# Attention windows and a highway layer on one core: the rectified product of eight tiles read by ScalarE, and a new order of the last two tiles

## The chip, the cores and the metric

The kernel runs on one core of a Trainium2 chip. The metric is the device time of one execution in microseconds (us), as the median of several runs. Five engines of the core work side by side, each through its own instructions in order: TensorE (PE in the profile, with its weight loads as PEld), VectorE (DVE), ScalarE (ACT), GpSimd (POOL) and SyncE (SP, here for stores only). They wait for one another through semaphores.

## The reference

Four batches of eight heads attend over 768 positions with 64 values a head. A position sees itself, the 127 before it, and the first four positions (the "sinks"). The heads' outputs, side by side, are the rows `x` of a highway layer:

```
scores = where(keep, scale * q @ k.T, -1e9)
x = softmax(scores) @ v                      # 3072 rows x 512
H = np.maximum(x @ w_h, 0.0)
T = 1.0 / (1.0 + np.exp(-(x @ w_t + b_t)))
out = T * H + (1.0 - T) * x
```

## The kernel before

The 3072 rows are 24 tiles of 128 rows, `N = 24`, six (`NC`) to a batch. All eight heads of a tile are worked on together. The last line of the reference is computed as `T * (max(h, 0) - x) + x`, where `h = x @ w_h`.

One tile goes through these steps, each a small function of the tile's number `n`:

- `scores(n)`: PE multiplies keys and queries into the PSUM tile `ps_s` (L303). `expo(n)`: ACT writes the exponentials to the fp16 tile `E` (L334). `mask(n)`: DVE multiplies `E` by a mask of ones and zeros (L342).
- `values(n)`: PE multiplies `E` of this tile and of the tile before by the values into `ps_v` (L371 and L374). A tile that begins a batch has no tile before it in its batch, so it has only the eight products of L374; the others have sixteen products, L371 and L374 in turn. L374 reads what `mask(n)` wrote.
- `norm(n)`: DVE takes reciprocals of the sums (L383) and writes the fp16 tile `X` (L384).
- `x_transpose(n)` on PE (L411) and `x_copy(n)` on ACT (L416) give the transposed rows `XT`.
- `bias(n)` and `gate(n)`: PE forms `x @ w_t + b_t` in `ps_z` (L421, L425). `tanh(n)`: ACT writes `TH = tanh(ps_z / 2)` (L449). The sigmoid is `0.5 * TH + 0.5`; that step is done on ACT by `gate_on_act` (L455) for the tiles that `on_act` names, and on POOL by `gate_value` (L460) for the others.
- `hidden(n)`: PE forms `x @ w_h` in `ps_h` (L465), in four products.
- `diff(n)`: one DVE instruction with `ps_h` and `X` as inputs writes `DD = max(ps_h, 0) - X` (L469). `gated(n)`: DVE multiplies `DD` by `TH` (L473). `add(n)`: POOL adds `X` (L477). `store(n)`: SP sends the tile to memory (L481).

The order of the work on every engine is the order in which the program is written. A loop at L657 makes one turn for each `s` from 5 to 21, and a turn works on five tiles at once, `n2 = s + 2` down to `n8 = s - 2`. In a turn, each engine's order is:

- PE: transposes of tile `n0 = s`, the last two products of `hidden(n9)` with `n9 = s - 1`, the scores of `n2`, the bias of `n0`, the values of `n1 = s + 1`, `gate(n0)`, the first two products of `hidden(n0)`.
- ACT: `x_copy(n0)`, `gate_on_act(n9)` where it is ACT's, `expo(n2)`, `tanh(n0)`.
- DVE: `mask(n1)`, `gated(n8)`, `diff(n9)`, `norm(n1)`, and in the turns 7 to 18 a transposition of query or key tiles (L155).
- POOL: `add(n8)`, `gate_value(n9)` where it is POOL's, in some turns the sink tables (L264, L280), and the loads that it issues (L130, L161).

In what follows "turn 12" means `s = 12`.

After the loop, the tiles 22 (`n0`) and 23 (`n1`) are finished by a sequence written out by hand (L705 to L747). The last tile is worked on in two halves of 256 columns, and its second half goes another way: two DVE instructions (L743, L745) and a store issued by ACT (L747).

Of the kernel before, what the change touches and what calls it, by code (L numbers as in the profile page):

```python
# [12 lines left out]
AF = mybir.ActivationFunctionType  # L13
ALU = mybir.AluOpType
# [16 lines left out]
def kernel(  # L31
# [14 lines left out]
    pe, act, dve, pool, sp = nc.tensor, nc.scalar, nc.vector, nc.gpsimd, nc.sync  # L46
# [10 lines left out]
    N = B * NC  # L57
# [237 lines left out]
    def scores(n):  # L295
        b, c = divmod(n, NC)
        nq = 2 if c + 1 < NC else 1
        new = n not in ADDED
        for hg in range(HG):
            for e in range(2):  # L300
                for g in range(G):
                    rows = slice(32 * g, 32 * g + 32)
                    pe.matmul(ps_s[:, g, hg, 0:nq * P],  # L303
                              lhsT=tr[b][rows, 1, hg, c * P:(c + 1) * P, e],
                              rhs=tr[b][rows, 0, hg, c * P:(c + nq) * P, e],
                              start=(new and e == 0), stop=(e == 1),
                              skip_group_check=not new)
# [16 lines left out]
    def sinks(b):  # L324
        sink_scores(b)
        sink_expo(b)
# [3 lines left out]
    def expo(n):  # L330
        c = n % NC
        nq = 2 if c + 1 < NC else 1
        E[n] = work.tile([P, G, HG, 2 * P], FP16, tag="E", name="E")
        act.activation(out=E[n][:, :, :, 0:nq * P], in_=ps_s[:, :, :, 0:nq * P],  # L334
                       func=AF.Exp, scale=SCALE)

    def mask(n):
        c = n % NC
        nq = 2 if c + 1 < NC else 1
        m = mask_0 if c == 0 else mask_std  # L340
        e3 = E[n].rearrange("p g hg x -> p (g hg) x")[:, :, 0:nq * P]
        return dve.tensor_tensor(  # L342
            out=e3, in0=e3, in1=m[:, 0:nq * P].unsqueeze(1).to_broadcast([P, H, nq * P]),
            op=ALU.mult)
# [7 lines left out]
    def values_of_sinks(n):  # L352
        b, t = divmod(n, NC)
        if t >= 2:
            rows = slice(32 * (t - 2), 32 * (t - 1))
            for i in range(2):
                pe.matmul(av_of(n)[:, i], lhsT=es[b % 2][rows],
                          rhs=vs[b][rows, HB * i:HB * i + HB, :].rearrange("p h e -> p (h e)"),
                          start=True, stop=False, skip_group_check=True)

    def values(n):
        b, t = divmod(n, NC)
        both = av_of(n)
        for i in range(2):
            for j in range(HB):
                h = HB * i + j
                g, hg = divmod(h, HG)
                slot = both[:, i, j * (D + 1):(j + 1) * (D + 1)]
                first = t < 2 and j == 0
                if t > 0:  # L370
                    pe.matmul(slot, lhsT=E[n - 1][:, g, hg, P:2 * P], rhs=v_of(n - 1)[:, h, :],  # L371
                              start=first, stop=False, skip_group_check=True)
                    first = False
                pe.matmul(slot, lhsT=E[n][:, g, hg, 0:P], rhs=v_of(n)[:, h, :],  # L374
                          start=first, stop=True, skip_group_check=True)

    X = [None] * N
# [12 lines left out]
    ALL = slice(0, DM)  # L390
    HALVES = [slice(0, DM // 2), slice(DM // 2, DM)]

    def z_of(n, cols):
        return ps_z[:, cols] if n < N - 1 or cols == HALVES[1] else ps_v[:, 0, cols]

    def h_of(n, cols):
        if n < N - 1 or cols == HALVES[1]:
            return ps_h[:, cols]
        return ps_s[:, 1].rearrange("p hg x -> p (hg x)")[:, cols]
# [6 lines left out]
    def flat(x):  # L406
        return x.rearrange("p i j d -> p (i j d)")

    def x_transpose(n):
        for kc in range(KC):  # L410
            pe.transpose(xt_of(n)[:, kc * P:(kc + 1) * P], flat(X[n])[:, kc * P:(kc + 1) * P],  # L411
                         ident)

    def x_copy(n):
        XT[n] = work.tile([P, KC * P], FP16, tag="XT", name="XT")
        act.copy(out=XT[n], in_=xt_of(n))  # L416

    def bias(n, cols=ALL, group=None):
        lhsT, rhs = (ones, brow) if group is None else (
            ones_g[32 * group:32 * group + 1], brow[32 * group:32 * group + 1])  # L420
        pe.matmul(z_of(n, cols), lhsT=lhsT, rhs=rhs[:, cols], start=True, stop=False)  # L421

    def gate(n, cols=ALL, parts=range(KC)):
        for kc in parts:
            pe.matmul(z_of(n, cols), lhsT=XT[n][:, kc * P:(kc + 1) * P], rhs=wt[:, kc, cols],  # L425
                      start=False, stop=(kc == KC - 1))

    TH = [None] * N
    DD = [None] * N
# [4 lines left out]
    def outputs(n):  # L434
        TH[n] = work.tile([P, DM], FP16, tag="TH", name="TH", bufs=6)
        DD[n] = work.tile([P, DM], FP16, tag="DD", name="DD", bufs=8)
        if O[n] is None:
            O[n] = work.tile([P, DM], FP32, tag="O", name="O", bufs=10)

    def on_act(n):  # L440

        return n < 6 or n in (8, 9, 12, 15, N - 3, N - 1)

    def at_once(n):

        return n < 6

    def tanh(n, cols=ALL, gate_too=True):
        act.activation(out=TH[n][:, cols], in_=z_of(n, cols), func=AF.Tanh, scale=0.5)  # L449
        if gate_too:  # L450
            gate_on_act(n, cols)

    def gate_on_act(n, cols=ALL):
        if on_act(n):
            act.activation(out=TH[n][:, cols], in_=TH[n][:, cols], func=AF.Copy, bias=0.5,  # L455
                           scale=0.5)

    def gate_value(n):
        if not on_act(n):
            pool.tensor_scalar(out=TH[n], in0=TH[n], scalar1=0.5, scalar2=0.5,  # L460
                               op0=ALU.mult, op1=ALU.add)

    def hidden(n, cols=ALL, parts=range(KC)):
        for kc in parts:
            pe.matmul(h_of(n, cols), lhsT=XT[n][:, kc * P:(kc + 1) * P], rhs=wh[:, kc, cols],  # L465
                      start=(kc == 0), stop=(kc == KC - 1))

    def diff(n, cols=ALL):
        dve.scalar_tensor_tensor(out=DD[n][:, cols], in0=h_of(n, cols), scalar=0.0,  # L469
                                 in1=flat(X[n])[:, cols], op0=ALU.max, op1=ALU.subtract)  # L470

    def gated(n, cols=ALL):
        return dve.tensor_tensor(out=DD[n][:, cols], in0=DD[n][:, cols], in1=TH[n][:, cols],  # L473
                                 op=ALU.mult)
# [182 lines left out]
    for s in range(5, N - 2):  # L657


        n2, n1, n0, n9, n8 = s + 2, s + 1, s, s - 1, s - 2  # L660
        x_transpose(n0)
        x_copy(n0)

        hidden(n9, parts=range(2, KC))
        if n2 % NC == 3:
            sinks(n2 // NC)
        if not at_once(n9):
            gate_on_act(n9)

        scores(n2)  # L670
        bias(n0, group=(n1 % NC + 1) % G)
        values_of_sinks(n1)
        expo(n2)

        if n1 not in ADDED:
            mask(n1)
        gated(n8)
        diff(n9)
        outputs(n0)
        values(n1)  # L680
        gate(n0, parts=range(0, 2))
        norm(n1)

        last = add(n8)
        while done < stored.get(n2, 0):
            store(done, after=last)
            done += 1
        gate_value(n9)
        if n2 in keys:
            sink_keys(keys[n2])  # L690
        if n2 in rows:
            sink_values(rows[n2], engine=pool)
        for load in loads[n2]:
            load()
        for piece in pieces[n2]:
            transpose_qk(*piece)
        for part in tiles[n2]:
            transpose_tiles(*part)
        if n2 == N - 1:
            mask(n2)  # L700
        gate(n0, parts=range(2, KC))
        tanh(n0, gate_too=at_once(n0))
        hidden(n0, parts=range(0, 2))

    n1, n0, n9, n8 = N - 1, N - 2, N - 3, N - 4  # L705
# [12 lines left out]
    gated(n9)  # L718
    finish(n9)
    gate(n0)  # L720
    tanh(n0)
    hidden(n0, parts=range(0, 1))
    x_transpose(n1)
    x_copy(n1)
    hidden(n0, parts=range(1, KC))
    gate_value(n0)
    diff(n0)
    gated(n0)
    finish(n0)
# [3 lines left out]
    for i, cols in enumerate(HALVES):  # L733
        gate(n1, cols)
        tanh(n1, cols, gate_too=(i == 0))
        hidden(n1, cols)
    diff(n1, HALVES[0])
    gated(n1, HALVES[0])
    finish(n1, HALVES[0])

    cols = HALVES[1]
    diff(n1, cols)
    dve.scalar_tensor_tensor(out=DD[n1][:, cols], in0=TH[n1][:, cols], scalar=1.0,  # L743
                             in1=DD[n1][:, cols], op0=ALU.add, op1=ALU.mult)
    dve.scalar_tensor_tensor(out=O[n1][:, cols], in0=DD[n1][:, cols], scalar=0.5,  # L745
                             in1=flat(X[n1])[:, cols], op0=ALU.mult, op1=ALU.add)
# [36 lines left out]
```

## Time and profile before

| what | us |
|---|---|
| median of 3 runs (110.75, 110.85, 113.58) | 110.85 |
| the profiled execution, its own time | 112.34 |
| its span from the first instruction to the last | 110.6 |
| DVE busy in the span | 94.9 |
| PE busy in the span | 97.8 |
| POOL busy in the span | 82.4 |
| ACT busy in the span | 79.4 |

The profiled execution's time has 1.74 us outside of its span, and it is 1.49 us above the median. The granted clock of TensorE has a mean of 0.975 of full speed over the span.

Each row of a timeline gives the start and the length in us, the engine, the line of the kernel, the operation, what is written `<-` what is read with shapes and types, the count, and in brackets how long the engine was idle before it and what ended the idle time. The rows of one engine can overlap by some 0.08 us, since the end of one instruction's writes lies beside the beginning of the next; the distance from start to start is then what an instruction costs its engine. The chain of waits goes back from the last instruction of the span to what released it, step by step.

### The profile page before, as it was taken

How to read it: one execution, taken by the hardware profiler on the slowest of the kernel's cores; microseconds unless marked ns; L12 is line 12 of the kernel's file. 1: busy time of each engine (PE TensorE's matmuls, PEld its weight loads, DVE VectorE, ACT ScalarE, POOL GpSimd, SP SyncE). 2: the span in 40 equal slices, each digit the busy share in tenths (PEclk: the TensorE clock that was granted, in tenths of full speed). 3: DMA queues.
4: the chain of work that ended last, by engine and by line, in shares of the span. 5: the costliest groups of instructions: out<-in, count | busy, mean ns of one | idle time of the engine just before them, and what ended most of it. 6: DMA issues, size and time to landing. Idle time of an engine off the chain costs nothing.

```text
span 110.6 us, 3031 instructions
## 1 busy us (share of the span) xinstructions
PE 97.8 (88%) x1199; PEld 51.4 (46%) x1199; DVE 94.9 (86%) x182; ACT 79.4 (72%) x105; POOL 82.4 (74%) x115
## 2 busy tenths in 40 slices
PE   5999777389999999899989999999999999999900
PEld 2344353246353654465445445655454555564600
DVE  5899889463989879999999999999989999899580
ACT  0934799806545989988959889988698879965700
POOL 6989995137989987689989799877995335664750
PEclk9999999967999999999999999999999999999996
DMA  3999999998999997999999999997999953345432
GB/s 95 251 211 168 141 183 165 184 202 131 119 168 166 126 144 68 152 106 115 128 121 94 162 273 154 171 267 160 186 150 203 232 190 115 121 147 191 182 128 69
DMA packets 45045, 17.53 MB, mean 158 GB/s; under 512 B 38500, under 2 KB 41316, under 8 KB 45032
## 3 DMA queue, kind: packets, MB, share of 16 engines
q0 software_dynamic: 40624, 9.97, 95.7%
q1 hardware_dynamic: 3944, 6.73, 17.1%
q10 hardware_dynamic: 464, 0.66, 2.2%
q8 instruction: 9, 0.15, 0.6%
q14 instruction: 4, 0.03, 0.1%
HBM read 21.01 MB, written 6.29 MB: 247 GB/s over the span
## 4 chain that ended last, share of the span: by engine, by line
PE 36%; DVE 35%; DMA 13%; issue 5%; POOL 5%; ACT 1%; DVEq 0%; POOLq 0%; ACTq 0%
DVE E L342 11%; PE ps_z L425 9%; DMA v<-in_v_dram 9%; PE ps_h L465 8%; DVE X L384 6%; DVE tr L155 5%; DMA nat<-in_q_dram 4%; DVE DD L469 4%; DVE DD L473 4%; PE ps_s L303 4%; PE ps_v L374 3%; PE ps_v L371 3%; PE ps_v L411 3%; DVE rec L383 2%; PE ps_z L421 2%
## 5 line engine op out<-in xcount | busy, mean ns | idle before, releaser
L334 ACT ACTIVATE E<-ps_s 128x2048 f16<-128x2048 f32 (+1 forms) x24 | 41.6, 1734 | 7.5 <-PE ps_s L303 7.5
L477 POOL TENSOR_TENSOR O<-DD,X 128x512 f32<-128x512 f16 (+1 forms) x19 | 21.4, 1128 | 14.3 <-DVE DD L473 14.2
L465 PE MATMUL ps_h<-wh,XT 128*128 128x512 f16 (+1 forms) x96 | 27.3, 375 | 0.0
L425 PE MATMUL ps_z<-wt,XT 128*128 128x512 f16 (+1 forms) x96 | 25.0, 384 | 0.0
L342 DVE TENSOR_TENSOR E<-E,mask_std 128x2048 f16<-128x2048 f16 (+1 forms) x19 | 22.0, 1157 | 0.7 <-ACT E L334 0.5
L449 ACT ACTIVATE TH<-ps_z 128x512 f16<-128x512 f32 (+1 forms) x24 | 14.1, 587 | 6.0 <-PE ps_z L425 6.0
L416 ACT COPY XT<-ps_v 128x512 f16<-128x512 f16 x23 | 13.4, 584 | 6.4 <-PE ps_v L411 5.4
L469 DVE SCALAR_TENSOR_TENSOR DD<-ps_h,X 128x512 f16<-128x512 f32 (+1 forms) x24 | 16.1, 671 | 1.2 <-PE ps_h L465 1.0
L384 DVE TENSOR_TENSOR X<-ps_v,rec 128x512 f16<-128x512 f32 x23 | 15.9, 691 | 1.0 <-DVE rec L383 0.2
L374 PE MATMUL ps_v<-v,E 128*128 128x65 f16 x184 | 13.6, 194 | 3.0 <-DMA v<-in_v_dram 1.8
L303 PE MATMUL ps_s<-tr 32*128 32x256 f16 (+1 forms) x384 | 14.5, 267 | 1.8 <-ACT E L334 1.6
L371 PEld LDWEIGHTS <-E 128*128 128x128 f16 x160 | 10.7, 97 | 6.5 <-issue 6.5
L371 PE MATMUL ps_v<-v,E 128*128 128x65 f16 x152 | 13.3, 195 | 0.3 <-ACT XT L416 0.3
L123 POOL DMA_DIRECT2D nat<-in_k_dram x16 | 8.9, 563 | 6.2 <-DMA v<-in_v_dram 3.5
L374 PEld LDWEIGHTS <-E 128*128 128x128 f16 x192 | 11.6, 98 | 3.8 <-DVE E L342 2.8
L161 POOL DMA_DIRECT2D v<-in_v_dram x11 | 13.1, 1187 | 0.2 <-ACT XT L416 0.2
L303 PEld LDWEIGHTS <-tr 32*128 32x128 f16 x384 | 8.1, 94 | 11.0 <-issue 6.6
L148 DVE STREAM_TRANSPOSE tr<-nat 128x512 f32<-128x512 f32 (+1 forms) x14 | 12.6, 943 | 0.5 <-DMA nat<-in_q_dram 0.3
L473 DVE TENSOR_TENSOR DD<-DD,TH 128x512 f16<-128x512 f16 (+1 forms) x24 | 11.3, 472 | 0.7 <-POOL TH L460 0.3
L425 PEld LDWEIGHTS <-XT 128*128 128x128 f16 x100 | 8.6, 99 | 6.7 <-issue 0.5
L465 PEld LDWEIGHTS <-XT 128*128 128x128 f16 x100 | 8.8, 98 | 5.8
L212 PE MATMUL ps_h<-zeros 128*128 128x512 f16 x33 | 10.1, 465 | 1.3 <-DVE ones_v L217 1.3
(88 smaller groups left out, 129.8 us busy)
## 6 DMA issues: line engine op xcount, KB each, us to landing
out_dram<-O SPq DMA_DIRECT2D x18, 256.0 KB
v<-in_v_dram POOLq DMA_DIRECT2D x11, 256.0 KB, 6.1
nat<-in_q_dram POOLq DMA_DIRECT2D x8, 192.0 KB, 4.1
nat<-in_k_dram POOLq DMA_DIRECT2D x8, 192.0 KB, 4.7
out_dram<-first SPq DMA_DIRECT2D x4, 256.0 KB
nat<-in_q_dram POOLq DMA_DIRECT2D x8, 96.0 KB, 7.7
nat<-in_k_dram POOLq DMA_DIRECT2D x8, 96.0 KB, 5.0
nat<-in_q_dram POOLq DMA_DIRECT2D x4, 128.0 KB, 4.6
```

Source lines behind the costliest of these rows:

```text
L303: pe.matmul(ps_s[:, g, hg, 0:nq * P], lhsT=tr[b][rows, 1, hg, c * P:(c + 1) * P, e], rhs=tr[b][rows, 0, hg, c * P:(c + nq) * P, e], start= ...
L334: act.activation(out=E[n][:, :, :, 0:nq * P], in_=ps_s[:, :, :, 0:nq * P], func=AF.Exp, scale=SCALE)
L342: return dve.tensor_tensor(out=e3, in0=e3, in1=m[:, 0:nq * P].unsqueeze(1).to_broadcast([P, H, nq * P]), op=ALU.mult)
L371: pe.matmul(slot, lhsT=E[n - 1][:, g, hg, P:2 * P], rhs=v_of(n - 1)[:, h, :], start=first, stop=False, skip_group_check=True)
L374: pe.matmul(slot, lhsT=E[n][:, g, hg, 0:P], rhs=v_of(n)[:, h, :], start=first, stop=True, skip_group_check=True)
L384: dve.tensor_tensor(out=X[n], in0=av[:, :, :, 0:D], in1=rec.unsqueeze(3).to_broadcast([P, 2, HB, D]), op=ALU.mult)
L425: pe.matmul(z_of(n, cols), lhsT=XT[n][:, kc * P:(kc + 1) * P], rhs=wt[:, kc, cols], start=False, stop=(kc == KC - 1))
L449: act.activation(out=TH[n][:, cols], in_=z_of(n, cols), func=AF.Tanh, scale=0.5)
L465: pe.matmul(h_of(n, cols), lhsT=XT[n][:, kc * P:(kc + 1) * P], rhs=wh[:, kc, cols], start=(kc == 0), stop=(kc == KC - 1))
L469: dve.scalar_tensor_tensor(out=DD[n][:, cols], in0=h_of(n, cols), scalar=0.0, in1=flat(X[n])[:, cols], op0=ALU.max, op1=ALU.subtract)
L473: return dve.tensor_tensor(out=DD[n][:, cols], in0=DD[n][:, cols], in1=TH[n][:, cols], op=ALU.mult)
L477: return pool.tensor_tensor(out=O[n][:, cols], in0=DD[n][:, cols], in1=flat(X[n])[:, cols], op=ALU.add)
```

## The change

For eight tiles (`TAKEN`: 7, 8, 10, 11, 13, 14, 16, 17) ACT reads `ps_h` and writes `max(ps_h, 0)` to `DD` as fp16 (`take_hidden`). In the turn's order on ACT this stands behind `x_copy(n0)` and `gate_on_act(n9)`, and ahead of `expo(n2)`. At the place of `diff`, DVE then subtracts `X` from `DD`, with both inputs in SBUF (`diff_of_taken`). These are the turns 8, 9, 11, 12, 14, 15, 17 and 18.

After the loop, the sigmoid step of tile 22 moves from POOL (`gate_value`) to ACT, behind `x_copy(23)`, and both halves of `diff(23)` stand ahead of the product with `TH` of the first half.

```diff
     def on_act(n):
 
-        return n < 6 or n in (8, 9, 12, 15, N - 3, N - 1)
+        return n < 6 or n in (8, 9, 12, 15) or n >= N - 3
...
+    TAKEN = (7, 8, 10, 11, 13, 14, 16, 17)
+
+    def take_hidden(n):
+        if n in TAKEN:
+            act.activation(out=DD[n], in_=h_of(n, ALL), func=AF.Relu)
+
+    def diff_of_taken(n):
+        dve.tensor_tensor(out=DD[n], in0=DD[n], in1=flat(X[n]), op=ALU.subtract)
...
         if not at_once(n9):
             gate_on_act(n9)
+        take_hidden(n9)
 
         scores(n2)
...
         gated(n8)
-        diff(n9)
+        if n9 in TAKEN:
+            diff_of_taken(n9)
+        else:
+            diff(n9)
         outputs(n0)
...
     gate(n0)
-    tanh(n0)
+    tanh(n0, gate_too=False)
     hidden(n0, parts=range(0, 1))
     x_transpose(n1)
     x_copy(n1)
     hidden(n0, parts=range(1, KC))
-    gate_value(n0)
+    gate_on_act(n0)
     diff(n0)
     gated(n0)
     finish(n0)
...
         gate(n1, cols)
         tanh(n1, cols, gate_too=(i == 0))
         hidden(n1, cols)
-    diff(n1, HALVES[0])
+        diff(n1, cols)
     gated(n1, HALVES[0])
     finish(n1, HALVES[0])
 
     cols = HALVES[1]
-    diff(n1, cols)
     dve.scalar_tensor_tensor(out=DD[n1][:, cols], in0=TH[n1][:, cols], scalar=1.0,
                              in1=DD[n1][:, cols], op0=ALU.add, op1=ALU.mult)
```

## The prediction

> **What bounds the kernel now.** I read the chain of waits first, then the timeline of one engine after the other. The chain (start, length, what):
>
> ```profile
> 75.66 1.12 DVE E L342
> 76.82 0.20 PE ps_v L374
> 77.46 0.86 PE ps_z L425 x4
> ```
>
> Up to this place the chain stays on DVE, turn after turn; here it leaves the mask for PE's values, and later, past 85 us, it runs through PE's products to the tail. So the eight turns lie mostly where DVE sets the pace, and what is won there counts if nothing else is late next. DVE's timeline for turn 12, mask to mask:
>
> ```profile
> 64.91 1.18 DVE L342 TENSOR_TENSOR E<-E,mask_std 128x2048 f16<-128x2048 f16 x1
> 66.01 0.41 DVE L473 TENSOR_TENSOR DD<-DD,TH 128x512 f16<-128x512 f16 x1
> 66.35 0.68 DVE L469 SCALAR_TENSOR_TENSOR DD<-ps_h,X 128x512 f16<-128x512 f32 x1
> 66.95 0.20 DVE L383 RECIPROCAL rec<-ps_v 128x8 f32<-128x8 f32 x1
> ...
> 68.41 1.18 DVE L342 TENSOR_TENSOR E<-E,mask_std 128x2048 f16<-128x2048 f16 x1
> ```
>
> No row has an idle time in brackets. A turn is 68.41 - 64.91 = 3.50 us. The gated product costs 0.34 us from start to start, the difference 0.60 us. Now PE's values and the reciprocals that read them, for turn 11 (which begins a batch), turn 12 and turn 16:
>
> ```profile
> 62.65 0.42 PE L374 MATMUL ps_v<-v,E 128*128 128x65 f16 x8
> ...
> 66.58 0.19 PE L374 MATMUL ps_v<-v,E 128*128 128x65 f16 x1
> ```
> ```profile
> 80.62 0.19 PE L374 MATMUL ps_v<-v,E 128*128 128x65 f16 x1
> ```
> ```profile
> 63.45 0.20 DVE L383 RECIPROCAL rec<-ps_v 128x8 f32<-128x8 f32 x1
> ...
> 80.92 0.21 DVE L383 RECIPROCAL rec<-ps_v 128x8 f32<-128x8 f32 x1 [0.25 <-PE ps_v L374]
> ```
>
> In turn 16 DVE did wait, and its reciprocal began 0.30 us after the start of the last L374. Put that on turn 12: 66.58 + 0.30 = 66.88, against 66.95 as it was. So behind the difference stands a second path, mask to values to reciprocal, only 0.07 us shorter. Turn 11 has half the products: its last one starts at 62.65 + 0.42 - 0.19 = 62.88, the reciprocal could start at 63.18 and does at 63.45, so there the room is 0.27 us. Turn 17 begins a batch as well.
>
> **The change: DVE.** The PSUM difference becomes an instruction of the gated product's form (two fp16 tiles in SBUF), so I take 0.34 us in place of 0.60: 0.26 us less, eight times, 2.1 us if all of it counted. It doesn't: a turn with sixteen products keeps 0.07 us, a turn with eight keeps 0.26 us.
>
> **ACT.** It gets eight reads of `ps_h`. The nearest rows are tanh (512 columns from PSUM) and the sigmoid step:
>
> ```profile
> 57.38 0.60 ACT L449 ACTIVATE TH<-ps_z 128x512 f16<-128x512 f32 x1 [1.12 <-PE ps_z L425]
> 58.05 0.58 ACT L416 COPY XT<-ps_v 128x512 f16<-128x512 f16 x1
> 58.53 0.63 ACT L455 ACTIVATE TH<-TH 128x512 f16<-128x512 f16 x1
> 59.06 1.88 ACT L334 ACTIVATE E<-ps_s 128x2048 f16<-128x2048 f32 x1
> ...
> 65.87 1.88 ACT L334 ACTIVATE E<-ps_s 128x2048 f16<-128x2048 f32 x1 [0.43 <-PE ps_s L303]
> ```
>
> One more such instruction takes 59.06 - 58.53 = 0.53 us. The cover is the gap ahead of the exponential, 0.43 us in turn 12 (and in 8, 11, 17, 18). So the exponential, queued behind it, is late by some 0.1 us, or by nothing if the read takes 0.45; the mask that wants it comes in the next turn, at 68.41, while the row ends at 65.87 + 1.88 = 67.75, with 0.66 us to spare. In turn 9 ACT has the sigmoid step as well and no gap, and the exponential moves by 0.53 us; but the tanh behind it waits 1.12 us for PE anyway (first row). I cost ACT at nothing; without the gap it would be 0.53 us a turn.
>
> **POOL.** This is where I expect the saving to go. Two SBUF inputs on DVE meet POOL's own reads:
>
> ```profile
> 54.08 0.62 POOL L460 TENSOR_SCALAR TH<-TH 128x512 f16<-128x512 f16 x1
> ...
> 66.51 1.15 POOL L477 TENSOR_TENSOR O<-DD,X 128x512 f32<-128x512 f16 x1 [0.34 <-DVE DD L473]
> 67.64 0.61 POOL L460 TENSOR_SCALAR TH<-TH 128x512 f16<-128x512 f16 x1
> ```
> ```profile
> 54.27 1.51 DVE L342 TENSOR_TENSOR E<-E,mask_std 128x2048 f16<-128x2048 f16 x1
> ```
>
> The mask that began beside POOL's sigmoid step (54.08 to 54.70) took 1.51 us, not 1.18: it was held for 0.33 us, to 54.60, that is until 0.10 before the row of POOL ends. The old difference has one input in SBUF, and ran beside the add of 66.51 at its usual 0.68. The new one has two. It starts 0.34 us after the gated product and POOL's add 0.50 us after it, so DVE comes first and the add is held. If POOL is let in when the new difference ends (0.34 + 0.41 = 0.75) or 0.10 before it (0.65), the add is late by d = 0.15 to 0.25 us; I take 0.2, since the one held row we have shows the early end. The sides: d = 0 if POOL isn't held, 0.35 if it restarts as much after the end as the mask did before it, 0.41 if it loses the whole instruction.
>
> Why it matters: behind the add comes POOL's sigmoid step, which now ends at 67.64 + 0.61 = 68.25, 0.16 us ahead of the mask at 68.41. Counted from the gated product, the mask now starts at 2.40 us; POOL would hold it until 68.25 - 0.10 - 66.01 = 2.14 + d; DVE alone would be ready at 2.33 (turn 12) or 2.14 (turn 11). So the later of the two sets the turn. With d = 0.2 a turn of either kind gains 0.06 us.
>
> The Trainium skill ("SBUF — State Buffer", section "SBUF: two separate sides") says that VectorE and GpSimd share a pair of ports as an exclusive lock, that a VectorE instruction with two SBUF inputs takes it against a GpSimd one that reads SBUF, and that the loser blocks for the whole instruction. The held mask agrees with it. By that rule taken strictly d is the 0.25 of the upper end above, and a turn gains 0.01 us.
>
> Which turns count: turn 8 doesn't, for the mask that follows it is the held one of 54.27, and POOL's row ends no sooner. Turn 9 is followed by a shorter mask and by reciprocals that wait for PE, turn 15 by the stretch in which the chain is on PE, and 18 lies in PE's stretch. That leaves 11, 12, 14 and 17: 4 x 0.06 = 0.24 us; ends, d = 0: 2 x 0.26 + 2 x 0.07 = 0.66 us gained; d = 0.41: 4 x 0.15 = 0.60 us lost.
>
> **The tail.** DVE, then POOL, PE and ACT:
>
> ```profile
> 103.16 0.69 DVE L469 SCALAR_TENSOR_TENSOR DD<-ps_h,X 128x512 f16<-128x512 f32 x1 [0.81 <-PE ps_h L465]
> 104.20 0.43 DVE L473 TENSOR_TENSOR DD<-DD,TH 128x512 f16<-128x512 f16 x1 [0.35 <-POOL TH L460]
> 104.54 0.42 DVE L469 SCALAR_TENSOR_TENSOR DD<-ps_s,X 128x256 f16<-128x256 f32 x1
> 105.06 0.94 DVE L473 TENSOR_TENSOR DD<-DD,TH 128x256 f16<-128x256 f16 x1
> 105.93 0.41 DVE L469 SCALAR_TENSOR_TENSOR DD<-ps_h,X 128x256 f16<-128x256 f32 x1
> 106.44 0.59 DVE L743 SCALAR_TENSOR_TENSOR DD<-TH,DD 128x256 f16<-128x256 f16 x1
> 107.07 0.42 DVE L745 SCALAR_TENSOR_TENSOR O<-DD,X 128x256 f32<-128x256 f16 x1
> ```
> ```profile
> 103.55 0.62 POOL L460 TENSOR_SCALAR TH<-TH 128x512 f16<-128x512 f16 x1
> 104.71 1.15 POOL L477 TENSOR_TENSOR O<-DD,X 128x512 f32<-128x512 f16 x1 [0.54 <-DVE DD L473]
> 106.08 0.67 POOL L477 TENSOR_TENSOR O<-DD,X 128x256 f32<-128x256 f16 x1 [0.23 <-DVE DD L473]
> ```
> ```profile
> 104.48 0.60 PE L465 MATMUL ps_h<-wh,XT 128*128 128x256 f16 x4
> ```
> ```profile
> 102.51 0.58 ACT L416 COPY XT<-ps_s 128x512 f16<-128x512 f16 x1
> ```
>
> The half-width gated product took 0.94 us, held by POOL's add until 105.86. In the new order: ACT's sigmoid step of tile 22 starts 0.48 us behind the copy and ends at 102.51 + 0.48 + 0.63 = 103.62. The gated product of tile 22 then waits only for its difference, 103.85 and the 0.10 us that DVE needs between a result and its reader (106.34 to 106.44): 103.95, not 104.20. POOL's add runs 0.51 later, 104.46 to 105.61. The second half's difference waits for PE (105.08) and runs from 105.14 to 105.55. The half gated product goes from about 105.5 to 105.8 (an estimate below the 0.41 of the full one). L743 is then free of POOL, 0.42 us as L745: to 106.2. POOL's last add, held by it, runs 106.2 to 106.87; L745 is held by that add to about 106.75 and ends at 107.15, not 107.49. That is 0.34 us less, and the last store goes out that much sooner; POOL's last half is 0.1 us later than now (106.75) but still ahead of it. Sides: 0.6 if POOL's add isn't held by L743, 0.1 if L745 or the half product is held longer.
>
> **Sum.** 0.24 + 0.34 = 0.58 us off the profiled execution, 112.34 to 111.8 (110.6 to 110.0 of span). Off the median of 110.85 it is 110.3.
>
> **Rivals.** (1) The lock costs more than the saving: POOL's add is late by 0.35 to 0.41 us, the mask is held each time, the loop loses 4 x 0.09 to 4 x 0.15 us, and the same holding eats the tail's gain down to 0.1. At the upper end 0.60 - 0.1 = 0.5 us slower: 111.35. It decides from d = 0.26 in the loop and, with the tail's 0.34, from d = 0.35 for the whole. For it: the margin of 0.16 us. Against: the early end of the held row. (2) POOL isn't held: 0.66 + 0.6 = 1.26 us, 109.6. Against: the held mask; for: that row shows DVE waiting, not POOL. (3) ACT becomes the bound: 8 x 0.53 = 4.2 us, 115.1; against it the gaps of 0.43 and 0.66 us. (4) The 0.30 us behind L374 is not a limit, and DVE keeps all of 8 x 0.26 = 2.1 us and 0.6 in the tail: 108.2; with a shorter wait still just over 2% is possible. (5) The new function needs its own table. The one load has this row:
>
> ```profile
> L208 ACT ACT_TABLE_LOAD x1 | 1.3, 1283 | 2.7 <-issue 2.7
> ```
>
> Two a turn in eight turns would be 16 x 1.28 = 20.5 us: 131. Exponential, tanh and copy run with this one load; whether a rectifier does, no row shows. The Trainium skill ("ScalarE: Activation LUTs", section "Table sets: the hidden batching unit") lists it in every set, so by that page there is no load; no run shown here has it.
>
> **Chances.** Forecast (d near 0.2) 0.50, at 110.3 with a range of its own of 109.9 to 110.7; (1) 0.24; (2) 0.16; (3) 0.04; (4) 0.04; (5) 0.02. The range from 109.5 to 111.4 holds the first three cases and leaves out the others, 0.10, with as much again for their edges. Over 2% (2.2 us, about what a measurement of this kernel can tell from no change) faster is case (4), 0.04; slower are (3) and (5), 0.06; the rest is 0.90.
>
> **What would show it.** The new difference at 0.41 us, in the turns 12 and 14 with idle time of about 0.1 us before the reciprocal, ended by L374; POOL's add starting over 0.6 us after the gated product; masks over 1.18 us beside POOL's sigmoid step in the turns 11 to 17; exponentials that lose their 0.43 us gap but are not waited for; the half gated product near 0.3 us and L745 held. I am wrong if the turns stay at 3.50 with no hold, if turns 12 and 14 shrink by over 0.1 us, or if ACT's exponential is what the mask waits for.

## The result

| | runs | median, us | range, us |
|---|---|---|---|
| before | 22 | 112.13 | 110.75 to 114.16 |
| changed | 22 | 111.37 | 109.63 to 113.59 |

The ratio of the changed kernel to the one before is 0.9892, with a 95% interval from 0.9847 to 0.9936: 1.2 us less, and between 0.7 and 1.7 us less. The ratio compares only the executions of each kernel that lie within 1.5% of its fastest, while the medians of the table are of all 22 and differ by 0.76 us. Single executions of either kernel lie up to 4 us apart, so the traces have to say where the time went.

The changed kernel's page, lines of busy time by engine (busy us, share of the span of 110.2 us, instructions):

```profile
PE 96.6 (88%) x1199; PEld 51.8 (47%) x1199; DVE 93.7 (85%) x182; ACT 83.1 (75%) x114; POOL 82.6 (75%) x114
```

ACT has 3.7 us more than before and DVE 1.2 us less. DVE's timeline of the changed kernel in turn 12, mask to mask:

```profile
65.01 1.29 DVE L342 TENSOR_TENSOR E<-E,mask_std 128x2048 f16<-128x2048 f16 x1
66.23 0.41 DVE L483 TENSOR_TENSOR DD<-DD,TH 128x512 f16<-128x512 f16 x1
66.56 0.41 DVE L480 TENSOR_TENSOR DD<-DD,X 128x512 f16<-128x512 f16 x1
67.03 0.21 DVE L383 RECIPROCAL rec<-ps_v 128x8 f32<-128x8 f32 x1
...
68.50 1.18 DVE L342 TENSOR_TENSOR E<-E,mask_std 128x2048 f16<-128x2048 f16 x1
```

The new difference (L480) is 0.41 us long where the old one was 0.68. The reciprocal now comes 0.80 us after the gated product (67.03 - 66.23), not 0.94. The first mask is 0.11 us longer than the second: it was held. What held it, on POOL at the end of turn 11:

```profile
63.37 1.27 POOL L487 TENSOR_TENSOR O<-DD,X 128x512 f32<-128x512 f16 x1 [0.49 <-DVE DD L483]
64.62 0.61 POOL L460 TENSOR_SCALAR TH<-TH 128x512 f16<-128x512 f16 x1
```

The add still starts 0.49 us after its gated product (62.88), but it takes 1.27 us where it took 1.15, since DVE's new difference is at work when it begins. Its delay, d in the prediction, is 0.12 us here and 0.11 us in turn 12, where the add takes 1.26 us. The sigmoid step behind it ends at 65.23, past the mask's start at 65.01. Now ACT in turn 12:

```profile
65.01 0.59 ACT L416 COPY XT<-ps_v 128x512 f16<-128x512 f16 x1
65.48 0.63 ACT L477 ACTIVATE DD<-ps_h 128x512 f16<-128x512 f32 x1
66.00 1.88 ACT L334 ACTIVATE E<-ps_s 128x2048 f16<-128x2048 f32 x1
```

The read of `ps_h` (L477) lies between the copy and the exponential, where a gap of 0.43 us had been; nothing on DVE waits for the exponential. No second table load appears.

The end of DVE's work, and POOL's last adds:

```profile
103.26 0.69 DVE L469 SCALAR_TENSOR_TENSOR DD<-ps_h,X 128x512 f16<-128x512 f32 x1 [0.81 <-PE ps_h L465]
104.06 0.42 DVE L483 TENSOR_TENSOR DD<-DD,TH 128x512 f16<-128x512 f16 x1
104.40 0.42 DVE L469 SCALAR_TENSOR_TENSOR DD<-ps_s,X 128x256 f16<-128x256 f32 x1
105.23 0.42 DVE L469 SCALAR_TENSOR_TENSOR DD<-ps_h,X 128x256 f16<-128x256 f32 x1 [0.41 <-PE ps_h L465]
105.57 0.29 DVE L483 TENSOR_TENSOR DD<-DD,TH 128x256 f16<-128x256 f16 x1
105.78 0.41 DVE L756 SCALAR_TENSOR_TENSOR DD<-TH,DD 128x256 f16<-128x256 f16 x1
106.23 0.77 DVE L758 SCALAR_TENSOR_TENSOR O<-DD,X 128x256 f32<-128x256 f16 x1
```
```profile
104.56 1.15 POOL L487 TENSOR_TENSOR O<-DD,X 128x512 f32<-128x512 f16 x1 [0.87 <-DVE DD L483]
105.94 0.78 POOL L487 TENSOR_TENSOR O<-DD,X 128x256 f32<-128x256 f16 x1 [0.23 <-DVE DD L483]
```

The half gated product takes 0.29 us in place of 0.94, as POOL's add is nearly over when it starts (105.57; the add's row ends at 105.71); the last instruction is now the one that is held (0.77 for 0.42). From the difference of tile 22 to the end of DVE's work the tail takes 3.74 us (107.00 - 103.26), before 4.33 (107.49 - 103.16): 0.59 us less.

In this execution the loop shows less than it could, for one wait of DVE (turn 15):

```profile
79.04 0.71 DVE L155 STREAM_TRANSPOSE tr<-nat 128x512 f32<-128x512 f32 x1 [0.57 <-DMA nat<-in_k_dram]
```

A load of keys, issued at 72.22 us, had not landed. One more fact about the span: the gated product of turn 8, which waits for none of the new ScalarE reads, comes at 52.25 us and before at 51.88, so this execution was 0.37 us behind already when the changed part began. That is why I compare stretches and not spans.

### The profile page after: what moved, and what is told of

Read it like the earlier page. It is cut to its first block, busy times and chain, and to the rows that moved or that the text cites. A ratio compares the mean times of both kernels' runs of the same rounds, so it can differ in the third digit from the quotient of the medians.

```text
span 110.2 us, 3033 instructions
## 1 busy us (share of the span) xinstructions
PE 96.6 (88%) x1199; PEld 51.8 (47%) x1199; DVE 93.7 (85%) x182; ACT 83.1 (75%) x114; POOL 82.6 (75%) x114
## 4 chain that ended last, share of the span: by engine, by line
PE 40%; DVE 22%; DMA 20%; POOL 7%; issue 4%; ACT 4%; DVEq 0%; POOLq 0%
PE ps_z L425 10%; DMA v<-in_v_dram 9%; PE ps_h L465 8%; DVE E L342 8%; DMA nat<-in_k_dram 6%; DVE tr L155 5%; DVE X L384 4%; DMA nat<-in_q_dram 4%; PE ps_v L374 4%; PE ps_v L371 4%; PE ps_s L303 4%; PE ps_z L421 2%; PE ps_v L411 2%; ACT E L334 2%; POOL nat L123 1%
## 5 line engine op out<-in xcount | busy, mean ns | idle before, releaser
L487 POOL TENSOR_TENSOR O<-DD,X 128x512 f32<-128x512 f16 (+1 forms) x19 | 22.3, 1175 | 13.6 <-DVE DD L483 13.4
L342 DVE TENSOR_TENSOR E<-E,mask_std 128x2048 f16<-128x2048 f16 (+1 forms) x19 | 22.5, 1185 | 0.7 <-ACT E L334 0.5
L374 PE MATMUL ps_v<-v,E 128*128 128x65 f16 x184 | 13.9, 196 | 3.5 <-DMA v<-in_v_dram 2.3
L371 PEld LDWEIGHTS <-E 128*128 128x128 f16 x160 | 11.0, 99 | 7.0 <-issue 7.0
L371 PE MATMUL ps_v<-v,E 128*128 128x65 f16 x152 | 13.6, 197 | 0.3 <-ACT XT L416 0.3
L374 PEld LDWEIGHTS <-E 128*128 128x128 f16 x192 | 11.9, 99 | 3.8 <-DVE E L342 3.1
L469 DVE SCALAR_TENSOR_TENSOR DD<-ps_h,X 128x512 f16<-128x512 f32 (+1 forms) x16 | 10.7, 668 | 1.5 <-PE ps_h L465 1.4
```

Source lines behind the costliest of these rows:

```text
L342: return dve.tensor_tensor(out=e3, in0=e3, in1=m[:, 0:nq * P].unsqueeze(1).to_broadcast([P, H, nq * P]), op=ALU.mult)
L487: return pool.tensor_tensor(out=O[n][:, cols], in0=DD[n][:, cols], in1=flat(X[n])[:, cols], op=ALU.add)
```

## The experiments

The table has the length of each turn, from the start of one gated product to the start of the next, worked out from DVE's timeline of each kernel's profile; then the stretch from the gated product of turn 8 to the difference of tile 22, and the tail as above. All in us.

| kernel | 8 | 9 | 10 | 11 | 12 | 13 | 14 | 15 | 16 | 17 | 18 | stretch | tail |
|---|---|---|---|---|---|---|---|---|---|---|---|---|---|
| before | 3.83 | 3.13 | 3.67 | 3.50 | 3.50 | 3.68 | 3.49 | 2.97 | 4.01 | 3.50 | 3.50 | 51.28 | 4.33 |
| changed | 3.83 | 3.25 | 3.55 | 3.35 | 3.38 | 3.73 | 3.39 | 3.52 | 3.70 | 3.35 | 3.38 | 51.01 | 3.74 |
| changed, again | 3.83 | 3.25 | 3.55 | 3.35 | 3.38 | 3.75 | 3.38 | 2.85 | 3.94 | 3.35 | 3.38 | 50.60 | 3.74 |
| loop only | 3.84 | 3.25 | 3.55 | 3.34 | 3.38 | 3.75 | 3.38 | 2.85 | 3.94 | 3.36 | 3.37 | 50.60 | 4.34 |
| tail only | 3.84 | 3.14 | 3.67 | 3.50 | 3.51 | 3.67 | 3.50 | 2.96 | 4.01 | 3.50 | 3.50 | 51.29 | 3.75 |
| read aside | 3.85 | 3.13 | 3.68 | 3.51 | 3.50 | 3.67 | 3.50 | 2.97 | 3.85 | 3.50 | 3.51 | 51.11 | 4.33 |
| no POOL sigmoid | 3.38 | 3.89 | 3.85 | 3.23 | 3.39 | 3.74 | 3.38 | 2.85 | 3.94 | 3.24 | 3.38 | 50.86 | 4.44 |
| half difference | 3.84 | 3.13 | 3.67 | 3.22 | 3.38 | 3.88 | 3.38 | 2.86 | 3.94 | 3.24 | 3.38 | 50.50 | 3.74 |
| four tiles | 3.83 | 3.14 | 3.68 | 3.35 | 3.37 | 3.75 | 3.38 | 2.97 | 3.85 | 3.34 | 3.50 | 50.64 | 3.74 |
| tile 7 swapped | 3.50 | 3.40 | 3.50 | 3.35 | 3.38 | 3.73 | 3.39 | 2.85 | 3.94 | 3.35 | 3.37 | 50.35 | 3.74 |

Turns that nothing was done to repeat to 0.02 us from kernel to kernel (turns 11 and 12 of "before" and "tail only"), while the whole times of one kernel differ by several us.

**The change in two parts, and once more.** "Loop only" has the eight tiles and the old tail, "tail only" the reverse:

```diff
# loop only, against the changed kernel
-        return n < 6 or n in (8, 9, 12, 15) or n >= N - 3
+        return n < 6 or n in (8, 9, 12, 15, N - 3, N - 1)
...
-    tanh(n0, gate_too=False)
+    tanh(n0)
...
-    gate_on_act(n0)
+    gate_value(n0)
     diff(n0)
...
-        diff(n1, cols)
+    diff(n1, HALVES[0])
...
     cols = HALVES[1]
+    diff(n1, cols)
```

> The eight tiles as in the change, the last two tiles as before. My theory: the loop and the tail each give a part of the gain. From gated product to gated product the turns 11, 12, 14 and 17 take 3.35 to 3.40 us (3.50 before), some 0.5 us together, less what a late load takes back; POOL's adds in these turns 1.26 us long; the tail from the difference of tile 22 to the end of the last DVE instruction 4.33 us, as before. Ratio 0.994 to 0.998. Rival, the tail carries all of it: ratio 1.000, the turns' gain lost again by turn 18. Rival, the loop carries all of it: ratio 0.989.

> The last two tiles as in the change, no tile's rectified product read by ScalarE. My theory: all turns as before (3.50 us), the tail 3.74 us in place of 4.33, which is 0.59 us off: ratio 0.994 to 0.996. Rival, the tail carries all of it: 0.989. Rival, the loop carries all: 1.000, the last store's landing takes the gain back.

> The change once more, on the same chip as its two parts. My theory: its gain is the sum of the two parts' gains to within 0.3 us, ratio 0.987 to 0.993. If the wait of the transposition of turn 15 for its load (0.57 us in the one profile there is) belongs to the change, it is there again; if it was an accident of that execution, turn 15 has no such wait. Rival, the parts share one gain: the ratio is that of the better part.

Measured: ratio 0.9956 (0.9901 to 1.0012) for the loop, 0.9987 (0.9925 to 1.0048) for the tail, 0.9824 (0.9751 to 0.9898) for both. For the tail and for both, the ratio lies outside of what was expected (0.994 to 0.996, and 0.987 to 0.993), though its interval reaches in. The intervals are too wide to add up the parts; they do exclude that the tail alone carries the gain. The turns settle it: the loop's part takes 0.68 us off the stretch (51.28 to 50.60) and leaves the tail at 4.34; the tail's part leaves the stretch at 51.29 and takes 0.58 off the tail; both together give 50.60 and 3.74. So 0.68 + 0.59 = 1.27 us, which lies in the interval of the ratio (0.7 to 1.7 us). The end of the span comes 3.16 us after DVE's last instruction with the change and 3.12 before, so the stores give back no more than 0.04 us of it.

Turn 15 has no wait for its load in either new profile, and the two turns 15 and 16 together take 6.79 us (6.98 before, 7.22 in the first profile). One of two profiles of the same kernel shows the late load, so it is not a fixed part of the change. Why it was late that time wasn't settled.

**ScalarE's read alone.** ACT reads `ps_h` into a tile that nobody uses, and DVE's old difference stands behind it.

```diff
+    def take_aside(n):
+        if n in TAKEN:
+            READ[n] = act.activation(out=aside, in_=h_of(n, ALL), func=AF.Relu)
...
             gate_on_act(n9)
+        take_aside(n9)
...
+            diff_behind(n9)      # L469 as before, made to wait for READ[n9]
```

> ScalarE reads the rectified product of the eight tiles into a tile that nobody uses; VectorE's difference reads PSUM as before, behind that read; the last tiles as before. My theory, ScalarE's read lies in a gap: turns as before, 3.50 us each, ratio 0.998 to 1.002. Rival, ScalarE becomes the bound: 0.1 to 0.5 us more in each of the eight turns, 0.8 to 4 us in all, ratio 1.007 to 1.04, with masks that wait for the exponential.

Measured: ratio 0.9951 (0.9899 to 1.0003), below the 0.998 to 1.002 expected, and beside 0.9956 for the loop's part: the times of these two kernels can't be told apart, so the turns have to. Every turn of the table but one lies within 0.02 us of before. ACT's timeline of this kernel in turn 12:

```profile
66.70 0.59 ACT L416 COPY XT<-ps_v 128x512 f16<-128x512 f16 x1
67.19 0.60 ACT L478 ACTIVATE aside<-ps_h 128x512 f16<-128x512 f32 x1
67.71 1.88 ACT L334 ACTIVATE E<-ps_s 128x2048 f16<-128x2048 f32 x1
```

The read costs 0.52 us from start to start and no turn gets longer: ACT is not the bound. The exception is turn 16, 3.85 us in place of 4.01. In the kernel before and in the three others whose loop is as before, `X` of turn 16 starts 0.20 us late behind its reciprocal; in this kernel and in all with the change in the loop it doesn't. The profile doesn't explain that wait, and I leave it open. It is worth some 0.16 us, and this kernel has that gain without any shorter difference.

The kernels from here on were executed once each, for the profile, except "tile 7 swapped"; they are read by their turns alone.

**POOL's sigmoid step left out.** Of the loop's part alone, without the step for seven tiles:

```diff
-        gate_value(n9)
+        if n9 not in TAKEN:
+            gate_value(n9)
```

> The loop's part of the change alone, with POOL's sigmoid step left out for seven of the eight tiles (7, 10, 11, 13, 14, 16, 17), so that POOL is not at work when the masks begin. Theory, POOL's port holds the mask: the masks behind the turns 11 and 17 go from 1.29 to 1.18 us, and these turns from 3.35 to 3.24; turn 8, whose mask took 1.63, goes from 3.83 to about 3.40; turns 12 and 14, whose masks are not held, stay at 3.38. Rival, the masks are long for another reason (ScalarE's exponential comes late): all turns as in the loop's part alone.

Measured: turn 8 3.38, turns 11 and 17 3.23 and 3.24, turns 12 and 14 unchanged; all masks of full width in these turns at 1.18. So POOL's sigmoid step is what holds the mask, in turns 11 and 17 for 0.11 us and in turn 8 for 0.45. The mask behind turn 8, in the changed kernel and here:

```profile
54.53 1.63 DVE L342 TENSOR_TENSOR E<-E,mask_std 128x2048 f16<-128x2048 f16 x1
```
```profile
52.40 1.18 DVE L342 TENSOR_TENSOR E<-E,mask_std 128x2048 f16<-128x2048 f16 x1
```

The stretch is not shorter for it, 50.86 against 50.60, because turn 9 is 0.64 us longer and turn 10 behind it 0.30, which I had not expected. DVE and POOL in turn 9:

```profile
53.50 0.42 DVE L483 TENSOR_TENSOR DD<-DD,TH 128x512 f16<-128x512 f16 x1
54.08 1.36 DVE L480 TENSOR_TENSOR DD<-DD,X 128x512 f16<-128x512 f16 x1 [0.16 <-ACT DD L477]
```
```profile
54.00 1.15 POOL L487 TENSOR_TENSOR O<-DD,X 128x512 f32<-128x512 f16 x1 [0.53 <-DVE DD L483]
```

With turn 8 shorter, the difference of turn 9 waits for ACT's read and starts 0.08 us after POOL's add, not before it. Now DVE is the one that is held, and for 0.94 us (1.36 - 0.42). In the changed kernel the difference comes first and POOL's add loses 0.11 us. Which of the two is first decides between these prices.

**Half of the difference.** The subtraction is done for half of the columns.

```diff
-        dve.tensor_tensor(out=DD[n], in0=DD[n], in1=flat(X[n]), op=ALU.subtract)
+        cols = HALVES[0]
+        dve.tensor_tensor(out=DD[n][:, cols], in0=DD[n][:, cols], in1=flat(X[n])[:, cols],
+                          op=ALU.subtract)
```

> The change, with VectorE's subtraction of the eight tiles done for half of the columns only, so that it costs 0.13 us less. Theory, the path from the mask through the values to the reciprocal is what is left in turns 12 and 14: they stay at 3.38 us; POOL's add is no longer held (1.15 in place of 1.26), so turns 11 and 17, bound by that hold, go from 3.35 to 3.24. Rival, VectorE's own work is still the bound: turns 11, 12, 14 and 17 all lose 0.13 us, to 3.22 to 3.25.

Measured: turns 12 and 14 stay at 3.38, turns 11 and 17 come to 3.22 and 3.24. DVE in turn 12:

```profile
64.14 0.41 DVE L485 TENSOR_TENSOR DD<-DD,TH 128x512 f16<-128x512 f16 x1
64.48 0.28 DVE L481 TENSOR_TENSOR DD<-DD,X 128x256 f16<-128x256 f16 x1
64.94 0.21 DVE L383 RECIPROCAL rec<-ps_v 128x8 f32<-128x8 f32 x1 [0.18 <-PE ps_v L374]
```

The 0.13 us saved became idle time in front of the reciprocal, which waits for L374. So in turns with sixteen products the path from mask to values to reciprocal is the bound, and DVE's work no longer is. Turn 13, where no tile was taken, is 0.13 us longer than in the changed kernel; why isn't shown. The last L374 of turn 12, here and in the changed kernel:

```profile
64.71 0.19 PE L374 MATMUL ps_v<-v,E 128*128 128x65 f16 x1
```
```profile
66.80 0.19 PE L374 MATMUL ps_v<-v,E 128*128 128x65 f16 x1
```

The reciprocals start 0.23 us behind them, at 64.94 and 67.03.

**Four tiles.** Only those that the prediction counted:

```diff
-    TAKEN = (7, 8, 10, 11, 13, 14, 16, 17)
+    TAKEN = (10, 11, 13, 16)
```

> The change with the tiles 10, 11, 13 and 16 alone (turns 11, 12, 14, 17). The prediction's list of turns that count: the stretch from the gated product of turn 8 to the difference of tile 22 is 50.60 us as with all eight (51.28 before), within 0.05. Rival, turns 15 and 18 count too, by 0.12 us each less what turn 19 gives back: 50.75 to 50.85. Turns 9 and 10 go back to 3.13 and 3.67.

Measured: 50.64 us. The four tiles give 0.64 of the 0.68 us; the other four add 0.04. Of the 0.64, 0.55 us lies in the turns 11, 12, 14 and 17, and 0.16 in turn 16, whose late `X` is gone here as in "read aside"; turn 13 takes 0.07 back. Turn 15 alone does gain 0.12 with its tile, and turn 16 gives 0.09 of it back (3.85 to 3.94), turn 18 likewise gives to turn 19.

**Tile 7 swapped.** What turn 8 lacks was shown above, with POOL's sigmoid step left out. ACT's load there is one instruction either way:

```diff
-        return n < 6 or n in (8, 9, 12, 15) or n >= N - 3
+        return n < 6 or n in (7, 8, 9, 12, 15) or n >= N - 3
...
-    TAKEN = (7, 8, 10, 11, 13, 14, 16, 17)
+    TAKEN = (8, 10, 11, 13, 14, 16, 17)
```

> The change, but for tile 7 ScalarE does the sigmoid step in place of POOL, and the rectified product stays with VectorE; ScalarE's load in turn 8 is the same. Theory: the mask behind turn 8 is held by POOL's sigmoid step of tile 7 and by nothing else, so turn 8 goes from 3.83 to about 3.50, and the stretch from the gated product of turn 8 to the difference of tile 22 from 50.60 to 50.25 or so; ratio to before 0.984 to 0.988. Rival: the next turns give it back (VectorE or POOL late in turns 9 and 10), stretch 50.60.

Measured: turn 8 3.50 as expected, turn 9 0.15 longer (its mask is held by the sink table, L280), turn 10 0.05 shorter; the stretch is 50.35, a gain of 0.25 us over the changed kernel in the trace, where I had expected 0.35. Its six runs have a median of 111.07 us beside 111.55 for the kernel before in the same job; that is a ratio of 0.996 where 0.984 to 0.988 was expected, and there is no interval for it. 0.25 us is too little for these times to show against the changed kernel. By its stretch and its tail it is the fastest of the versions that leave nothing out.

**The tail's two parts.** Each alone, on the kernel before; their edits are the tail's lines of the change.

> Of the tail's part only the move of tile 22's sigmoid step to ScalarE. Theory, the tail's gain is made of two holds that start earlier: from the difference of tile 22 to the end of the last VectorE instruction 4.08 us (4.33 before, 3.74 with both parts), all of it because the product of tile 22 and POOL's add behind it start 0.25 us sooner; the half product is still held by that add and takes about 0.9 us. Rival, the move gives nothing without the other part: 4.33.

> Of the tail's part only the order of the last tile's differences. Theory: the second difference runs while POOL's add holds the half product, so its 0.34 us leave the path: 4.00 us from the difference of tile 22 to the end (4.33 before). Rival, the half product is held by as much as before and the order gives nothing: 4.33; or it gives all of the 0.59: 3.74.

Measured: 4.09 us with the sigmoid step moved (107.87 - 103.78), 3.99 us with the new order (105.10 - 101.11). The parts are 0.24 and 0.34 and add up to 0.58. DVE with the new order alone:

```profile
103.07 0.42 DVE L469 SCALAR_TENSOR_TENSOR DD<-ps_h,X 128x256 f16<-128x256 f32 x1 [0.16 <-PE ps_h L465]
103.41 0.55 DVE L473 TENSOR_TENSOR DD<-DD,TH 128x256 f16<-128x256 f16 x1
103.88 0.41 DVE L742 SCALAR_TENSOR_TENSOR DD<-TH,DD 128x256 f16<-128x256 f16 x1
104.33 0.77 DVE L744 SCALAR_TENSOR_TENSOR O<-DD,X 128x256 f32<-128x256 f16 x1
```

The half product is still held by POOL's add, but only to 0.55 us, since the second difference fills part of the hold.

## Why the prediction held, and where its sizes were off

The time moved the way that was forecast, and the range held it. That the median lies in it is luck: 111.37 us is 0.03 us inside the upper end, because the kernel before came out at 112.13 over 22 runs where the forecast had started from 110.85. Counted as a gain, the 1.2 us lies inside the range (1.35 us gained to 0.55 lost) but outside of the forecast's own (0.15 to 0.95 gained). The forecast of 0.58 us was about half of the 1.27 us that the stretches show. Step by step:

- **What the turn is made of: right.** Four tiles give 0.64 of 0.68 us ("four tiles"), 0.55 of it in the turns the prediction named, and turn 8 gives nothing because its mask is held. The 0.16 us of turn 16 was not foreseen, and its cause is open.
- **ACT at nothing: right.** "Read aside" has the read, and no turn is longer. The cover is thin in one place: with turn 8 made shorter ("no POOL sigmoid"), the difference of turn 9 waits 0.16 us for the read.
- **The second path, mask to values to reciprocal: right as a mechanism, mis-sized.** "Half difference" shows it as the bound of turns 12 and 14. The prediction took 0.30 us from the start of the last L374 to the reciprocal, from one row of turn 16, and so left 0.07 us to gain. Turn 16 is of another kind: every kernel has 0.29 or 0.30 us in the turns 13, 16 and 19, but the kernels with the change in the loop have 0.23 in the turns 12 and 14. In "half difference", where the reciprocal visibly waits, it is 64.94 - 64.71, and in the changed kernel 67.03 - 66.80. So these two turns gained 0.12 and 0.11 us, where the prediction let this path give 0.07 at most.
- **POOL held by the new difference: right, mis-sized.** d is 0.11 to 0.12 us, not 0.2. POOL's add starts 0.49 us after the gated product, and 0.11 more ends at 0.60, which is 0.15 us before the row of the new difference ends (0.33 + 0.42). The prediction let DVE go 0.10 before at the earliest, and took the middle. A turn that begins a batch therefore gained 0.26 - 0.11 = 0.15 us, and not 0.06. With 2 x 0.15 + 0.12 + 0.11 the four turns come to 0.53 us in place of 0.24; what the stretch has beyond that is mostly turns 15 and 16 (0.19 together, with the open 0.16 of turn 16 in it), less 0.07 lost in turn 13, where the last L374 starts 1.97 us after the mask (70.47 - 68.50), and 1.88 us in the kernel before (70.29 - 68.41).
- **The tail: right in order, mis-sized.** The prediction had POOL's last add held until L743 ended at 106.2, and from there the last instruction until 107.15; in this execution, which is 0.10 us behind, that would be 106.30 and 107.25. L743 (now L756) ended at 106.19, as the half product cost 0.21 us from start to start and not about 0.3. And the add was held for 0.11 us only (0.78 in place of 0.67), to 106.05, which is 0.14 us before that end. The two make the 0.25 us by which the last instruction ended sooner, at 107.00: 0.59 us in place of 0.34.
- **Signs of being wrong.** Two went against the prediction. It called itself wrong if turns 12 and 14 shrank by over 0.1 us, and they shrank by 0.12 and 0.11: the second path had more room than it had read. And POOL's add did not start over 0.6 us after the gated product; it started 0.49 us after it, as before, and took longer.
- **The rivals.** A hold dearer than the saving did not come, as d stayed below 0.26 us. An unheld POOL is excluded by the adds of 1.26 us, though its time, 1.26 us off, was nearer to the measured one than the forecast. ScalarE as the bound is excluded by "read aside", all of VectorE's 2.1 us by "half difference", and the table load by the single load in the changed kernel's profile.

The Trainium skill's rule of an exclusive port pair ("SBUF — State Buffer", section "SBUF: two separate sides") agrees with the order of the two holds here: the one who starts first runs at its own length, and the other is held, POOL for 0.11 us or DVE for 0.94. The strict end of the rule, a hold for the whole instruction, does not: by it d would have been 0.25.

## What to carry to other kernels

When an instruction on a full engine is shortened, look for the second path that ends at the same place; here the products between mask and reciprocal left about half of each 0.26 us, and the half difference shows in one run that more shortening buys only idle time. When an operand moves from PSUM to SBUF, list what the other engine reads from SBUF at that moment (here POOL) and who of the two starts first: when DVE was second it lost 0.94 us, and when it was first POOL lost 0.11. And where executions differ by more than the effect, measure from an event behind the disturbance to one at the end.

## What the runs showed of the hardware

What happens ahead of the loop spreads the executions far more than the change moves them. The gated product of turn 8 comes at 49.82 us in the profile of the tail's new order and at 53.69 us in "read aside", 3.87 us apart with the same work ahead of it on DVE, and three times the 1.27 us of the change. Between 16 and 30 us, PE waited 3.3 us for loads of `v` in "read aside" and 1.0 us in the other; from 22 to 28 us the granted clock was 0.50 in "read aside" and 1.00 in the other, and the four products of one `gate` took 1.71 us in place of 0.86. From there to the difference of tile 22, kernels whose loop was not edited differ by 0.03 us (51.28 before, 51.31 with the sigmoid step of tile 22 moved).

In the turns of the table and in the tail, a DVE instruction that reads two tiles of SBUF and a POOL instruction that reads SBUF did not run side by side, and both let go a little before their rows end: POOL 0.10 us (the mask of 54.27 in the kernel before) to 0.14 (the half product of 105.06 there), DVE 0.14 to 0.15 us (d and the tail above). In turn 9 of "tile 7 swapped" POOL's add starts 0.01 us after DVE's difference and takes 1.42 us in place of 1.15: it loses 0.27 us of a row of 0.42. So the second one loses what is left of the other's row, less that little.

The rows don't always tell who is second. Ahead of the loop, in "tail only", a gated product starts 0.15 us before POOL's add and takes 1.62 us in place of 0.41 all the same:

```profile
36.85 1.62 DVE L473 TENSOR_TENSOR DD<-DD,TH 128x512 f16<-128x512 f16 x1
```
```profile
37.00 1.17 POOL L477 TENSOR_TENSOR first<-DD,X 128x512 f32<-128x512 f16 x1
```

POOL had just issued a load there (35.81 to 36.98). Why DVE was the one held isn't shown, and at 1.21 us it is the dearest hold of a DVE product or mask in these profiles.
